# Inverse square roots of two layer norms: one GpSimd power instruction in place of an integer seed and Newton steps

## The chip, the core and the metric

The kernel runs on one core of a Trainium2 chip. Its time is device time in microseconds (us); the figure for a kernel is the median of its runs. A profile is one execution recorded by the hardware profiler; its times count from the start of its span. Engines are named as in the profile: PE (TensorE, matmuls), PEld (TensorE's weight loads), DVE (VectorE), ACT (ScalarE), POOL (GpSimd) and SP (SyncE, which issues nearly all transfers here).

## What is computed

One decode step of a transformer block: one row of 512 numbers, with two pieces. Piece A normalises the row, multiplies by wq to 32 query heads, attends over a cache of 16384 keys and values for 8 heads (four query heads share one), and multiplies by wo. Piece B normalises again and runs an MLP. With a sequence of length 1, the padded and shifted parts of B's mixer are all zero, so w1 and w2 have no effect and x1 is B's input.

```python
def _layernorm(x, axis=-1, eps=1e-5):
    m = jnp.mean(x, axis=axis, keepdims=True)
    v = jnp.var(x, axis=axis, keepdims=True)
    return (x - m) / jnp.sqrt(v + eps)
...
h = x + _A_ref(_layernorm(x, axis=-1), A_k_cache, A_v_cache, A_wq, A_wo)
h2 = h + _B_ref(_layernorm(h, axis=-1), B_w1, B_w2, B_w3, B_w4)
# _B_ref(x) comes down to: x + _gelu(_layernorm(x) @ w3) @ w4
```

In the second place two layer norms follow each other: B's input is the layer norm of h, and the MLP normalises that again. The mean of the second is zero and its variance is v/(v + eps), so both come from one variance v. The kernel keeps two inverse roots for it: number 0, of v + eps, for the residual (h + layernorm(h)), and number 1, of v(1 + eps) + eps², as the scale of the gelu's input.

## The kernel before, in words

**The stream.** SP issues every large transfer in a fixed order: wq (4 MB, into vb), then for four pairs of key/value heads the keys in two halves (kb[0], kb[1], 4 MB each) and the values (vb, 8 MB; the last pair's in two parts), then wo in four pieces (into kb[0]) and w3 in three and w4 in four pieces (into kb[1]). An issue waits until the buffer that it overwrites has been read: a key half until DVE has transposed it into kt (L609), a value block until PE has used it (L662), the first value block until the queries are computed from wq (L586). The pieces of w4 (`W4`) are row blocks 0 to 4, 5 to 9, 10 to 12 and 13 of 14.

**Start, first layer norm.** POOL makes an identity matrix (L545), DVE casts a corner of it (L550) and spreads it (L551), and PE uses it to bring x into rows of 128 on all partitions (L553). `row_sums` (L478) gives sum and sum of squares; `variance` (L496) the negative of the squared-mean difference, clamped; `seeds` (L505) adds epsilon (L513) and makes a first guess of the inverse root by integer arithmetic on the bits (L515, L518); `inverse_root` (L521) halves the argument (L528) and runs three Newton steps of two instructions each (L531, L533). All of it runs on DVE, on 128 partitions by 1 column. Meanwhile POOL clears two tiles, qb and pt (L560, L561). DVE then makes masks (L563 to L574) and, once wq has landed, the normalised input xn (L577), which starts the queries (L586).

**Attention.** For each pair DVE transposes the keys, PE forms the scores (L626), ACT takes the exponentials (L647), DVE transposes them (L651), and PE multiplies by the values (L662). POOL does nothing here but wait for the values (L448).

**End, second layer norm.** PE multiplies by wo (L728), DVE and PE fold the four partial rows (L732, L734), and `row_sums` forms h (tile hr) and its sums. ACT writes the centred row hc (L740); PE multiplies it by w3 (L746) without waiting for the scale. In that time DVE computes the variance, both arguments (L513 twice), both seeds and the Newton steps of root 1, and POOL the steps of root 0; POOL then forms xs = (h - mean) times root 0 (L753) and xsum = h + xs (L755). ACT's gelu (L758) needs the w3 product and root 1 as its scale; it runs in two halves, each transposed by DVE into hcol (L762). PE multiplies by w4 (L772), four matmuls for each of the 14 row blocks, block by block; ahead of block 10 it adds xsum through an identity matmul (L768). ACT writes the row (L777) and SP stores it (L778).

**Order.** Each engine runs its instructions in the order in which the program adds them. Semaphore waits are put in where an instruction reads or overwrites what another engine, or an earlier instruction of its own, has written. `dve`, `pool`, `act` and `pe` (L458 to L469) add an instruction to an engine's list.

Of the kernel before, what the change touches and what calls it, by code (L numbers as in the profile page):

```python
# [6 lines left out]
FP32 = mybir.dt.float32  # L7
BF16 = mybir.dt.bfloat16
I32 = mybir.dt.int32
ALU = mybir.AluOpType  # L10
# [331 lines left out]
def bass_sequential_preLN__gqa_block_cached__mixer_s_mlp__decode_kernel(  # L342
# [13 lines left out]
    with ExitStack() as ctx:  # L356
        sb = lambda name, shape, dt: ctx.enter_context(nc.sbuf_tensor(name, shape, dt))
# [26 lines left out]
        zd = sb("zd", [128, 32], FP32)  # L384
        scr = sb("scr", [128, 4], FP32)
        st = [sb(f"st{i}", [128, 16], FP32) for i in range(2)]
        sti = [sb(f"sti{i}", [128, 4], I32) for i in range(2)]
        xn = sb("xn", [128, NCH], BF16)
        qcol = sb("qcol", [128, 4, PAIRS * REP, 32], FP32)
        qb = sb("qb", [128, 4, PAIRS, QW], BF16)  # L390
# [15 lines left out]
        hr = sb("hr", [128, 128], FP32)  # L406
# [3 lines left out]
        xs = sb("xs", [128, 128], FP32)  # L410
        xsum = sb("xsum", [128, 128], FP32)
# [46 lines left out]
        def dve(fn, r=(), w=(), bank=()):  # L458
            return P.op("DVE", fn, r, w, bank)

        def act(fn, r=(), w=(), bank=()):
            return P.op("ACT", fn, r, w, bank)

        def pool(fn, r=(), w=(), bank=()):
            return P.op("POOL", fn, r, w, bank)
# [5 lines left out]
        def piece(cuts, m):  # L471
            return [lo <= m < hi for lo, hi in cuts].index(True)
# [23 lines left out]
        def variance(i):  # L496

            s, S = st[i], ("st", i)

            dve(lambda e: e.scalar_tensor_tensor(s[:, 2:3], s[:, 0:1], s[:, 0:1], s[:, 1:2],  # L500
                                                 ALU.mult, ALU.add), r=[(S, 0)], w=[(S, 2)])
            dve(lambda e: e.tensor_scalar(s[:, 3:4], s[:, 2:3], 0.0, -1.0, ALU.min, ALU.mult),
                r=[(S, 2)], w=[(S, 3)])

        def seeds(i, ns):  # L505


            s, t = st[i], sti[i]
            S, T = ("st", i), ("sti", i)
            lo, hi = min(ns), max(ns) + 1  # L510
            for n in ns:
                mul, add = (1.0 + EPS, EPS * EPS) if n else (1.0, EPS)
                dve(lambda e, n=n, mul=mul, add=add: e.tensor_scalar(s[:, 4 + n:5 + n], s[:, 3:4], mul, add,  # L513
                                                                     ALU.mult, ALU.add), r=[(S, 3)], w=[(S, 4 + n)])
            dve(lambda e: e.tensor_single_scalar(t[:, 2 + lo:2 + hi], s[:, 4 + lo:4 + hi].bitcast(I32), 1,  # L515
                                                 ALU.arith_shift_right),
                r=[(S, 4 + n) for n in ns], w=[(T, 2)])
            dve(lambda e: e.tensor_scalar(t[:, lo:hi], t[:, 2 + lo:2 + hi], -1, 1597463007,  # L518
                                          ALU.mult, ALU.add), r=[(T, 2)], w=[(T, n) for n in ns])

        def inverse_root(i, n, by):  # L521

            s, t = st[i], sti[i]
            S, T = ("st", i), ("sti", i)
            v, y = s[:, 4 + n:5 + n], t[:, n:n + 1].bitcast(FP32)
            z = s[:, 8 + n:9 + n]
            vh = s[:, 10 + n:11 + n]
            by(lambda e: e.tensor_scalar(vh, v, -0.5, None, ALU.mult), r=[(S, 4 + n)], w=[(S, 10 + n)])  # L528
            for k in range(3):
                dst, key = (s[:, 6 + n:7 + n], (S, 6 + n)) if k == 2 else (y, (T, n))  # L530
                by(lambda e: e.tensor_scalar(z, y, y, vh, ALU.mult, ALU.mult),  # L531
                   r=[(T, n), (S, 10 + n)], w=[(S, 8 + n)])
                by(lambda e, dst=dst: (e.scalar_tensor_tensor if by is dve else e.tensor_scalar)(  # L533
                    dst, z, 1.5, y, ALU.add, ALU.mult),
                   r=[(S, 8 + n), (T, n)], w=[key])


        load("x4", x4[:, :], A_x[0, 0:1, :].rearrange("o (q j) -> (o q) j", q=4), "x4", "ACT")
# [8 lines left out]
                                               channel_multiplier=1), r=["ident_f"], w=["ident_f"])  # L547


        dve(lambda e: e.tensor_copy(ident[:, :], ident_f[0:4, 0:4]), r=["ident_f"], w=["ident"])  # L550
        dve(lambda e: e.tensor_copy(quarter[:, :, :], ident[:, :].unsqueeze(2).to_broadcast([4, 4, 32])),  # L551
            r=["ident", "x4"], w=["quarter"])
        pe(lambda e: e.matmul(O_ps[0][:, 0:128], quarter[:, :, :].rearrange("p q u -> p (q u)"), x4[:, :],  # L553
                              start=True, stop=True), r=["quarter"], w=[("O", 0)], bank=[("O", 0)])
        row_sums(0, O_ps[0], ("O", 0))
        variance(0)
        seeds(0, (0,))
        inverse_root(0, 0, dve)
        act(lambda e: e.activation(scr[0:1, 0:1], mean4[0:1, 0:1], ACTF.Exp), r=["mean4"], w=["scr"])
        pool(lambda e: e.memset(qb[:, :, :, :], 0.0), w=["qb"])  # L560
        pool(lambda e: e.memset(pt[:, :, :, :, :], 0.0), w=["pt"])  # L561
# [2 lines left out]
            r=["ident_f"], w=["row32"])  # L564
        dve(lambda e: e.tensor_reduce(maskdd[:, :], ident_f[:, :].rearrange("p (n d) -> p d n", d=4), AX.X, ALU.add),
            r=["ident_f"], w=["maskdd"])
# [6 lines left out]
        for z, m, key, mk in ((zo, rowgh, "zo", "rowgh"), (zd, maskgh, "zd", "maskgh")):  # L573
# [5 lines left out]
            r=["hT", (("st", 0), 0), (("st", 0), 6)] + [("v", x) for x in range(VP)], w=["xn"])  # L579
# [3 lines left out]
        for i, key in enumerate(keys):  # L583
            P.part("query", i)
            for k in range(NCH):
                pe(lambda e, k=k: e.matmul(row[:, bass.ds(P.b, 512)], copies(xn[:, k:k + 1], 128),  # L586
                                           wq_k[:, k, bass.ds(P.c, REP * DH)], start=(k == 0), stop=(k == NCH - 1)),
                   r=["xn"], also=[("v", x) for x in range(VP)], w=["n" if key == "mn" else key], bank=[key])
        P.part()
        for g in range(2):  # L590
            half = banks[64 * g:64 * g + 64, PAIRS * g:PAIRS * g + PAIRS, :].rearrange("p j c -> p (j c)")
            for b in range(2):
# [3 lines left out]
                    r=["n" if x == "mn" else x for x in keys[PAIRS * g:PAIRS * g + PAIRS]], w=["qcol"],  # L596
                    bank=keys[PAIRS * g:PAIRS * g + PAIRS])
        for a in range(4):
            lo, hi, at = 32 * a, 32 * a + 32, QPAD + 32 * a
# [118 lines left out]
        for n, (lo, hi) in enumerate(W4):  # L718
# [4 lines left out]
            r=["o_m"], w=["o_f"])  # L723
        dve(lambda e: e.tensor_copy(o_b[:, :], o_f[:, :]), r=["o_f", ("r", 0, 0)], w=["o_b"])  # L724

        for r_ in range(32):
# [3 lines left out]
               r=["o_b"] + [("r", 0, n) for n in (piece(WO, r_),) if n], w=[("O", 0)], bank=[("O", 0)])  # L730
        h_ps, hkey = banks[:, 6, :], "spare0"
        dve(lambda e: e.tensor_copy(osum[:, :], O_ps[0][:, :]), r=[("O", 0)], w=["osum"], bank=[("O", 0)])  # L732
        for q in range(4):
            pe(lambda e, q=q: e.matmul(h_ps[32 * q:32 * q + 32, 0:128], copies(row32[:, 0:1], 32),  # L734
                                       osum[:, q * 128:(q + 1) * 128], start=True, stop=True),
               r=["osum", "row32"], w=[hkey], bank=[hkey])
        s = st[1]
        S = ("st", 1)
        row_sums(1, h_ps, hkey)
        act(lambda e: e.activation(hc[:, :, :], hT[:, :, :], ACTF.Identity, bias=s[:, 0:1], scale=1.0),  # L740
            r=["hT", (S, 0)] + [("r", 1, 0)], w=["hc"])


        for k in range(NCH):
            for q in range(4):
                pe(lambda e, k=k, q=q: e.matmul(s_ps[32 * q:32 * q + 32, 0, 0:FQ], hc[:, k, :],  # L746
                                                w3_sb[:, k, q * FQ:(q + 1) * FQ], start=(k == 0), stop=(k == NCH - 1)),
                   r=["hc"] + [("r", 1, n) for n in (piece(W3, k),) if n], w=[("s", 0)], bank=[("s", 0)])
        variance(1)
        seeds(1, (0, 1))  # L750
        inverse_root(1, 1, dve)
        inverse_root(1, 0, pool)
        pool(lambda e: e.tensor_scalar(xs[:, :], hr[:, :], s[:, 0:1], s[:, 6:7], ALU.add, ALU.mult),  # L753
            r=["hr", (S, 0), (S, 6)], w=["xs"])
        pool(lambda e: e.tensor_tensor(xsum[:, :], hr[:, :], xs[:, :], ALU.add), r=["hr", "xs"], w=["xsum"])  # L755
        for n in range(2):
            lo, hi = n * NHC // 2, (n + 1) * NHC // 2
            act(lambda e, lo=lo, hi=hi: e.activation(  # L758
# [7 lines left out]
        for m in range(NHC):  # L766
# [4 lines left out]
            for o in range(4):  # L771
# [4 lines left out]
                   r=[("hcol", 2 * m // NHC), ("r", 1, len(W3) + piece(W4, m))], w=["n"], bank=["mn"])  # L776
        act(lambda e: e.activation(fin[:, :], n_ps[:, 0:128], ACTF.Identity), r=["n"], w=["fin"], bank=["mn"])  # L777
        P.op("SP", lambda e: e.dma_start(out[0, 0:1, :].rearrange("o (q j) -> (o q) j", q=4), fin[0:128:32, :]),  # L778
             r=["fin"], w=["out"], dma="out")
# [32 lines left out]
```

## Time and profile before

| | |
|---|---|
| median of 3 runs | 191.78 us (191.37 to 191.93) |
| profiled execution, span | 190.4 us, 2182 instructions |
| what lies around the span | about 1.4 us (median less span; the profiled execution's own time is not listed apart) |
| PE busy | 118.6 us (62%) |
| DVE busy | 118.2 us (62%), 155 instructions |
| ACT busy | 9.3 us (5%) |
| POOL busy | 7.3 us (4%), 16 instructions |
| read from HBM | 79.17 MB, 416 GB/s over the span |

A row of the timeline gives start, duration, engine, line, operation, the tile written and the tiles read, the shape, and the number of instructions merged into it; in brackets stands the time that the engine was idle before it, and what ended that. A row of a group of instructions gives its busy time, the mean duration of one in ns, and its idle time with the releaser.

### The profile page before, as it was taken

The numbers are of one execution on the slowest core, as the hardware profiler recorded it, in microseconds if no ns is written. First come the engines' busy times: TensorE is split into PE (matmuls) and PEld (weight loads), VectorE is DVE, ScalarE is ACT, GpSimd is POOL, SyncE is SP. The second block draws the span as 40 slices with busy tenths as digits, with TensorE's granted clock in tenths as the row PEclk, the third lists the DMA queues.
The fourth block names the chain that finished last, engine by engine and source line by source line (L and its number), as shares of the span: only waits on it lengthen the run. The fifth ranks groups of instructions, "written<-read, shape, count | busy, mean of one in ns | idle before, by whom it ended". The sixth has DMA issues, their size and how long they took to land.

```text
span 190.4 us, 2182 instructions
## 1 busy us (share of the span) xinstructions
PE 118.6 (62%) x695; PEld 46.1 (24%) x695; DVE 118.2 (62%) x155; ACT 9.3 (5%) x16; POOL 7.3 (4%) x16
## 2 busy tenths in 40 slices
PE   0119709996195599940944989508449995294644
PEld 0103203442031143310311433203113332031212
DVE  6740799995504989845049989350479895504370
ACT  3000000000200000011000000020000000500020
POOL 7100000000000000000000000000000000000060
PEclk9999985899958579995585899975979999758855
DMA  6999999999999999997999999979999999989991
GB/s 227 434 441 441 441 441 441 441 441 441 413 441 406 420 523 441 441 441 330 441 441 441 523 441 413 441 324 420 413 441 441 441 441 441 441 367 421 409 411 51
DMA packets 3619, 79.20 MB, mean 416 GB/s; under 512 B 416, under 2 KB 544, under 8 KB 1568
## 3 DMA queue, kind: packets, MB, share of 16 engines
q1 hardware_dynamic: 3608, 79.17, 97.2%
q8 instruction: 1, 0.02, 0.0%
q14 instruction: 2, 0.02, 0.0%
q10 hardware_dynamic: 8, 0.00, 0.0%
HBM read 79.17 MB, written 0.00 MB: 416 GB/s over the span
## 4 chain that ended last, share of the span: by engine, by line
PE 39%; DMA 37%; DVE 16%; issue 4%; ACT 2%; ACTq 0%; SPq 0%; DVEq 0%
DMA kb<-in_A_k_cache_dram 31%; PE banks L626 22%; PE banks L662 6%; DMA vb<-in_A_wq_dram 6%; DVE kt L609 6%; PE banks L586 5%; DVE pt L651 3%; PE banks L728 2%; DVE mx L636 1%; ACT p_sb L647 1%; PE banks L620 1%; DVE od L681 1%; PE banks L772 1%; DVE qcol L593 1%; PE banks L639 1%
## 5 line engine op out<-in xcount | busy, mean ns | idle before, releaser
L609 DVE STREAM_TRANSPOSE kt<-kb 128x2048 int32<-128x2048 int32 (+1 forms) x37 | 71.3, 1987 | 4.3 <-DMA kb<-in_A_k_cache_dram 2.8
L626 PE MATMUL banks<-kt,qn 128*128 x256 | 68.7, 414 | 0.5
L626 PEld LDWEIGHTS banks<-kt,qn 128*128 x256 | 26.2, 102 | 41.4 <-issue 24.6
L662 PE MATMUL banks<-vb,pt 128*32 128x512 bf16 x256 | 24.4, 565 | 2.8 <-POOLq L448 2.8
L678 DVE TENSOR_SCALAR od<-banks,rowc 128x128 f32<-128x128 f32 x4 | 1.4, 350 | 26.3 <-PE banks L662 26.3
L620 PE MATMUL banks<-qn 128*128 128x512 bf16 x8 | 4.0, 495 | 17.3 <-DVE kt L609 17.1
L651 DVE STREAM_TRANSPOSE pt<-p_sb 64x1024 bf16<-64x1024 bf16 x8 | 9.9, 1239 | 5.4 <-ACT p_sb L647 5.3
L662 PEld LDWEIGHTS banks<-vb,pt 128*32 128x32 bf16 x256 | 9.0, 136 | 16.4 <-issue 12.4
L586 PE MATMUL banks<-vb,xn 128*128 x32 | 8.9, 446 | 6.1 <-DVE xn L577 6.1
L669 PE MATMUL banks<-acc,zd 128*32 128x1 f32 x8 | 1.1, 202 | 17.7 <-DVE pt L651 17.7
L647 ACT ACTIVATE p_sb<-banks,bias 128x1024 bf16<-128x1024 f32 x4 | 4.5, 1113 | 155.4 <-DVE nmh L643 155.4
L636 DVE TENSOR_REDUCE mx<-banks 128x1 f32<-128x1024 f32 x4 | 4.9, 1224 | 8.1 <-PE banks L626 8.1
L593 DVE STREAM_TRANSPOSE qcol<-banks 64x1024 f32<-64x1024 f32 x4 | 4.8, 1226 | 6.9 <-PE banks L586 6.9
L528 POOL TENSOR_SCALAR st<-st 128x1 f32<-128x1 f32 x1 | 0.2, 241 | 176.1 <-DVE st L513 176.1
L586 PEld LDWEIGHTS banks<-vb,xn 128*128 128x128 bf16 x32 | 3.6, 112 | 11.0 <-issue 8.5
L639 PE MATMUL banks<-mxd,mean 128*128 128x128 f32 x8 | 2.0, 326 | 6.6 <-DVE mxd L637 6.6
L620 PEld LDWEIGHTS banks<-qn 128*128 128x128 bf16 x8 | 0.8, 100 | 20.2 <-issue 20.0
L684 PE MATMUL banks<-od,zo 128*32 128x128 f32 x8 | 1.6, 285 | 6.5 <-DVE od L681 6.5
L669 PEld LDWEIGHTS banks<-acc,zd 128*32 128x32 f32 x8 | 0.7, 140 | 18.4 <-DVE pt L651 18.4
L681 DVE SCALAR_TENSOR_TENSOR od<-banks,rowc,od 128x128 f32<-128x128 f32 x12 | 4.2, 351 | 0.4
L550 DVE CAST ident<-ident_f 4x4 bf16<-4x4 f32 x1 | 3.8, 3848 | 0.6 <-POOL ident_f L545 0.6
L728 PE MATMUL banks<-kb,o_b 128*32 128x512 bf16 x32 | 3.5, 583 | 1.1 <-DVE o_b L724 1.1
(78 smaller groups left out, 44.6 us busy)
## 6 DMA issues: line engine op xcount, KB each, us to landing
kb<-in_A_k_cache_dram SPq DMA_DIRECT2D x8, 4096.0 KB, 29.7
vb<-in_A_v_cache_dram SPq DMA_DIRECT2D x2, 4096.0 KB, 29.2
vb<-in_A_wq_dram SPq DMA_DIRECT2D x1, 4096.0 KB, 12.3
kb<-in_A_wo_dram SPq DMA_DIRECT2D x2, 1536.0 KB, 25.4
kb<-in_B_w_dram SPq DMA_DIRECT2D x2, 640.0 KB, 25.4
kb<-in_B_w_dram SPq DMA_DIRECT2D x1, 896.0 KB, 22.4
kb<-in_B_w_dram SPq DMA_DIRECT2D x2, 448.0 KB, 23.4
kb<-in_A_wo_dram SPq DMA_DIRECT2D x1, 768.0 KB, 28.5
```

Source lines behind the costliest of these rows:

```text
L586: pe(lambda e, k=k: e.matmul(row[:, bass.ds(P.b, 512)], copies(xn[:, k:k + 1], 128), wq_k[:, k, bass.ds(P.c, REP * DH)], start=(k == 0), s ...
L593: dve(lambda e, g=g, b=b, half=half: e.transpose(qcol[64 * g:64 * g + 64, 2 * b:2 * b + 2, :, :].rearrange("p e m u -> p (e m u)"), half.r ...
L609: P.op("DVE", lambda e, view=view: e.transpose(view(kt), view(kb[y])), r=[("r", y, i) for i in range(RPARTS)], w=[("kt", t + i) for i in r ...
L620: pe(lambda e: e.matmul(row[:, bass.ds(P.y, 512)], copies(none, 128), copies(none, 512), start=True, stop=False, skip_group_check=True), r ...
L626: pe(lambda e, n=n: e.matmul(row[:, bass.ds(P.y, 512)], qn[:, n, bass.ds(P.q, 128)], key_piece(P.k, n), start=False, stop=(n == 3), skip_g ...
L636: dve(lambda e: e.tensor_reduce(mx[:, :], s_all, AX.X, ALU.max), r=[("s", 0), ("s", 1)], w=["mx"], **both)
L639: pe(lambda e: e.matmul(m_ps[:, 0:128], mean4[:, :], mxd[:, :], start=True, stop=True), r=["mxd", "mean4"], w=["m"], bank=["mn"])
L647: act(lambda e: e.activation(p_sb[:, :], s_all, ACTF.Exp, bias=bias[:, 0:1], scale=float(SCALE), accum_out=acc[:, :]), r=[("s", 0), ("s", ...
L651: dve(lambda e, g=g: e.transpose(pt[64 * g:64 * g + 64, :, :, g, :], p_sb[64 * g:64 * g + 64, :]), r=["p"], w=["pt"])
L662: pe(lambda e, l=l, ct=ct, ch=ch: e.matmul(O_ps[0][32 * ct:32 * ct + 32, :], pt[:, l, ch, :, :].rearrange("p g u -> p (g u)"), tiles[:, l ...
L681: dve(lambda e, block=block, c=c: e.scalar_tensor_tensor(od[:, :], block, rowc[:, c:c + 1], od[:, :], ALU.mult, ALU.add), r=[key, "rowc", ...
L728: pe(lambda e, r_=r_, q=q: e.matmul(O_ps[0][32 * q:32 * q + 32, :], copies(o_b[:, r_:r_ + 1], 32), wo_sb[:, r_ * D:(r_ + 1) * D], start=(r ...
```

## The change

The seeds and the Newton steps go, and with them the tile sti. `variance` now also makes the arguments, and one POOL instruction raises them to the power -0.5, with a tile of exponents (expo, 128x2, all -0.5, set by POOL at the start): 128x1 in the first layer norm, 128x2 in the second, where both roots come from one instruction. In the first layer norm that instruction stands on POOL ahead of the clearing of qb and pt. In the second, DVE forms xs as h - mean, without the root, and xsum as xs times root 0 plus h; POOL keeps only the power. The gelu and xsum wait for POOL. In the changed kernel the lines after the removed functions have smaller numbers.

```diff
-        sti = [sb(f"sti{i}", [128, 4], I32) for i in range(2)]
+        expo = sb("expo", [128, 2], FP32)
...
             dve(lambda e: e.tensor_scalar(s[:, 3:4], s[:, 2:3], 0.0, -1.0, ALU.min, ALU.mult),
                 r=[(S, 2)], w=[(S, 3)])
-        def seeds(i, ns):
...
+            for n in range(1 + i):
                 mul, add = (1.0 + EPS, EPS * EPS) if n else (1.0, EPS)
                 dve(lambda e, n=n, mul=mul, add=add: e.tensor_scalar(s[:, 4 + n:5 + n], s[:, 3:4], mul, add,
                                                                      ALU.mult, ALU.add), r=[(S, 3)], w=[(S, 4 + n)])
...
-        def inverse_root(i, n, by):
...
+            pool(lambda e: e.tensor_tensor(s[:, 6:7 + i], s[:, 4:5 + i], expo[:, 0:1 + i], ALU.pow),
+                 r=["expo"] + [(S, 4 + n) for n in range(1 + i)], w=[(S, 6 + n) for n in range(1 + i)])
...
+        pool(lambda e: e.memset(expo[:, :], -0.5), w=["expo"])
         dve(lambda e: e.tensor_copy(ident[:, :], ident_f[0:4, 0:4]), r=["ident_f"], w=["ident"])
...
         variance(0)
-        seeds(0, (0,))
-        inverse_root(0, 0, dve)
         act(lambda e: e.activation(scr[0:1, 0:1], mean4[0:1, 0:1], ACTF.Exp), r=["mean4"], w=["scr"])
         pool(lambda e: e.memset(qb[:, :, :, :], 0.0), w=["qb"])
         pool(lambda e: e.memset(pt[:, :, :, :, :], 0.0), w=["pt"])
...
         variance(1)
-        seeds(1, (0, 1))
-        inverse_root(1, 1, dve)
-        inverse_root(1, 0, pool)
-        pool(lambda e: e.tensor_scalar(xs[:, :], hr[:, :], s[:, 0:1], s[:, 6:7], ALU.add, ALU.mult),
-            r=["hr", (S, 0), (S, 6)], w=["xs"])
-        pool(lambda e: e.tensor_tensor(xsum[:, :], hr[:, :], xs[:, :], ALU.add), r=["hr", "xs"], w=["xsum"])
+        dve(lambda e: e.tensor_scalar(xs[:, :], hr[:, :], s[:, 0:1], None, ALU.add), r=["hr", (S, 0)], w=["xs"])
+        dve(lambda e: e.scalar_tensor_tensor(xsum[:, :], xs[:, :], s[:, 6:7], hr[:, :], ALU.mult, ALU.add),
+            r=["hr", "xs", (S, 6)], w=["xsum"])
```

More of the change, by code (lines that the diff above doesn't have):

```diff
@@ L503, in variance @@
                 r=[(S, 2)], w=[(S, 3)])
-        def seeds(i, ns):
[L508 to L511, printed above, removed]
+            for n in range(1 + i):
                 mul, add = (1.0 + EPS, EPS * EPS) if n else (1.0, EPS)
@@ L514, in seeds @@
                                                                      ALU.mult, ALU.add), r=[(S, 3)], w=[(S, 4 + n)])
[L515 to L519, printed above, removed]
-        def inverse_root(i, n, by):
[L523 to L535, printed above, removed]
+            pool(lambda e: e.tensor_tensor(s[:, 6:7 + i], s[:, 4:5 + i], expo[:, 0:1 + i], ALU.pow),
+                 r=["expo"] + [(S, 4 + n) for n in range(1 + i)], w=[(S, 6 + n) for n in range(1 + i)])
         load("x4", x4[:, :], A_x[0, 0:1, :].rearrange("o (q j) -> (o q) j", q=4), "x4", "ACT")
```

## The prediction

> **What bounds the kernel now.** I read the page first, for the span, the DMA row and the GB/s row.
>
> ```profile
> span 190.4 us, 2182 instructions
> DMA  6999999999999999997999999979999999989991
> GB/s 227 434 441 441 441 441 441 441 441 441 413 441 406 420 523 441 441 441 330 441 441 441 523 441 413 441 324 420 413 441 441 441 441 441 441 367 421 409 411 51
> ```
>
> The third line gives the DMA traffic in 40 slices of 4.76 us. After the start-up slice most slices stand near 440 GB/s (the lowest at 324), the 39th is still at 411, and only the last one falls to 51. The transfers run through from the first microseconds to within 4 us of the end: the kernel is a stream of 79 MB, and computation costs time only where it follows the last transfers. So the next view is the timeline of the tail, where the second layer norm lies. Columns are start, duration, engine, line and operation; in brackets, the engine's idle time before it and what ended that.
>
> ```profile
> 181.56 0.21 DVE L513 TENSOR_SCALAR st<-st 128x1 f32<-128x1 f32 x2
> 181.57 1.68 PE L746 MATMUL banks<-kb,hc 128*32 128x448 bf16 x16 [0.69 <-ACT hc L740]
> 181.80 0.24 POOL L528 TENSOR_SCALAR st<-st 128x1 f32<-128x1 f32 x1 [176.12 <-DVE st L513]
> 182.59 0.11 PEld L746 LDWEIGHTS banks<-kb,hc 128*32 128x32 bf16 x4 [0.52 <-DMA kb<-in_B_w_dram]
> 183.61 0.19 DVE L533 SCALAR_TENSOR_TENSOR st<-st,sti 128x1 f32<-128x1 f32 x1
> 183.89 0.85 ACT L758 ACTIVATE hg<-banks,st 128x224 bf16<-128x224 f32 x2 [2.37 <-DVE st L533]
> 184.33 0.26 POOL L533 TENSOR_SCALAR st<-st,sti 128x1 f32<-128x1 f32 x1
> 184.41 1.04 DVE L762 STREAM_TRANSPOSE hcol<-hg 128x224 bf16<-128x224 bf16 x2 [0.61 <-ACT hg L758]
> 185.04 0.46 PEld L772 LDWEIGHTS banks<-kb,hcol 128*32 128x32 bf16 x20 [2.33 <-DVE hcol L762]
> 185.04 1.45 PE L772 MATMUL banks<-kb,hcol 128*32 128x128 bf16 x40 [1.79 <-DVE hcol L762]
> 185.22 0.45 POOL L755 TENSOR_TENSOR xsum<-hr,xs 128x128 f32<-128x128 f32 x1
> 185.76 0.46 PEld L772 LDWEIGHTS banks<-kb,hcol 128*32 128x32 bf16 x20 [0.26 <-DMA kb<-in_B_w_dram]
> 186.41 0.50 PEld L768 LDWEIGHTS banks<-xsum,ident_f 128*128 128x128 f32 x2 [0.20 <-issue]
> 187.14 0.62 PE L772 MATMUL banks<-kb,hcol 128*32 128x128 bf16 x16
> 187.81 0.28 ACT L777 ACTIVATE fin<-banks 128x128 bf16<-128x128 f32 x1 [3.08 <-PE banks L772]
> 188.12 0.63 SPq L778 DMA_DIRECT2D out_dram<-fin  x1
> ```
>
> Three things are to be seen. First, the Newton steps do end a wait: L533 is done at 183.61 + 0.19 = 183.80 and the gelu (L758) starts 0.09 later, at 183.89, while the matmuls that it also needs (L746) end at 181.57 + 1.68 = 183.25. Second, a later wait ends on something else. The first 20 weight loads of L772 (blocks m = 0 to 4, four each) start at 185.04, but the next 20 (m = 5 to 9) start at 185.76 after 0.26 us idle that a transfer into kb ended: the second piece of W4 (blocks 5 to 9) had not landed. Third, from 185.76 nothing waits for the layer norm any more: 20 matmuls, the residual's matmul (L768, at 186.41; its operand xsum was ready at 185.22 + 0.45 = 185.67), the last 16 matmuls from 187.14, the last activation at 187.81, the output DMA at 188.12, and 190.4 - 188.12 = 2.3 us for that to finish.
>
> Are those transfers late because of the arithmetic, or because of the stream? Two more views answer it: the issues by line (the last two numbers are first and last start) and the windows of the tail (last two columns: DMA share and GB/s).
>
> ```profile
> L433 SPq DMA_DIRECT2D kb<-in_B_w_dram x7: 328/432/5845, 157.9 to 168.8; - x7
> 184.00:185.00 1.00, 0.00 (x0) 0.00 (x0) 0.59 (x2) 0.74 (x2) 0.80 (x3) 0.50 0.96 389
> 185.00:186.00 1.00, 0.96 (x32) 0.70 (x36) 0.45 (x1) 0.00 (x0) 0.59 (x2) 0.50 1.01 390
> 186.00:186.50 0.50, 0.50 (x21) 0.30 (x10) 0.00 (x0) 0.00 (x0) 0.00 (x0) 0.50 0.48 164
> 186.50:187.00 0.50, 0.50 (x2) 0.42 (x2) 0.00 (x0) 0.00 (x0) 0.00 (x0) 0.50 0.05 18
> ```
>
> All seven weight transfers of the second block were issued by 168.8, 17 us before the wait, and the DMA engines are still fully busy (0.96 and 1.01) while PE waits; they run empty in the half microsecond after 186. The landing at 185.7 is therefore set by the bytes ahead in the queue, and no edit of a layer norm moves it. That is the bound against which this change must be held.
>
> **The change, second layer norm.** Removed on DVE, after L513: L515, L518, L528 and three pairs L531/L533, nine instructions, from 181.56 + 0.21 = 181.77 to 183.80, 2.03 us. Removed on POOL: L528 and three pairs (n = 0), L753 and L755. Added: one POOL power over two columns, 128x2, which now stands alone between L513 and the gelu; call its duration P. DVE gets two 128x128 operations, xs (needs no root) and xsum (needs it).
>
> Start of the power: POOL's L528 started at 181.80, 0.09 after the first of the two L513 ended (181.56 + 0.15, by its row below), which is the one it needs; the power needs the second, so 181.77 + 0.09 = 181.86. Gelu start: 181.86 + P + 0.09 (the same handover as from DVE to ACT) = 181.95 + P, and not before 183.30 (end of L746 and 0.05).
>
> Gain side: at P up to 1.35 the gelu starts at 183.30, 0.59 sooner than now. Blocks 0 to 4 then run from 184.45, and PE waits for the second W4 piece 0.26 + 0.59 = 0.85 us instead of 0.26. Everything from 185.76 on stays. The whole 0.59 goes into that wait: gain 0.
>
> Loss side: the gelu may start 0.26 later than now, at 184.15, before blocks 5 to 9 start later. So the break-even is P = 184.15 - 181.95 = 2.20 us, and beyond it each microsecond of P is a microsecond of the kernel. DVE's new xsum waits for the power too, and ahead of hcol in the queue; it takes about 0.3 (L637 below has its shape), and the gelu's first half, which hcol waits for, takes 0.85/2 = 0.43 and its handover: the gelu covers it, barely. If it didn't, hcol would be some 0.1 us later, which the 0.26 takes up while P stays under about 2.1.
>
> How long is P? No power instruction stands in the trace. The nearest rows, with busy time and mean ns of one:
>
> ```profile
> L531 POOL TENSOR_SCALAR st<-sti,st 128x1 f32<-128x1 f32 x3 | 1.0, 340 | 0.4 <-DVE st L528 0.2
> L533 POOL TENSOR_SCALAR sti<-st,sti 128x1 f32<-128x1 f32 x2 | 0.5, 264 | 0.2
> L755 POOL TENSOR_TENSOR xsum<-hr,xs 128x128 f32<-128x128 f32 x1 | 0.5, 453 | 0.1
> L528 POOL TENSOR_SCALAR st<-st 128x1 f32<-128x1 f32 x1 | 0.2, 241 | 176.1 <-DVE st L513 176.1
> L531 DVE TENSOR_SCALAR st<-sti,st 128x1 f32<-128x1 f32 x6 | 1.6, 273 | 0.2
> L637 DVE TENSOR_SCALAR mxd<-ident_f,mx 128x128 f32<-128x128 f32 x4 | 1.1, 287 | 0.1
> L513 DVE TENSOR_SCALAR st<-st 128x1 f32<-128x1 f32 x3 | 0.4, 150 | 0.1
> ```
>
> Lower end: 0.24, one simple POOL instruction on one column (L528). Nearest in kind: 0.45, a POOL TENSOR_TENSOR over 128 columns (L755); the power has two columns, but more arithmetic in each. Upper end: the seven POOL steps that compute one root in the rows above run from 181.80 to 184.33 + 0.26 = 184.59, 2.79 us; a power done in software as laboriously, one column after the other, would take twice that, 5.6. I take 0.45, by the row that is of the same engine and instruction, and keep 0.24 and 5.6 for the range. The sum is 0 for every P up to 2.20; at 5.6 it is +3.4.
>
> One sharing could move the break-even: xs on DVE and the power on POOL become ready together. In the rows above a 128x128 TENSOR_SCALAR takes 287 ns and a 128x1 one (L513) 150: 137 ns for 127 more columns, about 1.08 ns each. I read that as one column per step, without a faster mode, so that xs leaves POOL alone and the break-even stays at 2.20.
>
> The Trainium skill, "SBUF — State Buffer", section "Who interferes with whom", says that a VectorE tensor_scalar between SBUF tensors can enter a mode that takes the port pair it shares with GpSimd, and that whichever starts first then blocks the other for its whole instruction; by that rule the power would start up to 0.29 late and the break-even would be 1.91. The skill's "VectorE: DVE Perf Modes", section "Side-by-side: where the cycles go for N=2048 bf16", puts an element at one cycle of 0.96 GHz without that mode, an estimate of 1.04 ns; the 1.08 of the rows agrees with it.
>
> **The change, first layer norm.** Nine DVE instructions leave here too, and the power (128x1) is put ahead of POOL's two memsets.
>
> ```profile
> 1.53 0.29 POOL L545 TENSOR_SCALAR_AFFINE_SELECT ident_f<-ident_f 128x128 f32<-128x128 f32 x1 [1.11 <-DVE ident_f L544]
> 1.76 2.18 POOL L560 MEMSET qb<- 128x2496 bf16 x1
> 1.86 3.85 DVE L550 CAST ident<-ident_f 4x4 bf16<-4x4 f32 x1 [0.57 <-POOL ident_f L545]
> 3.88 1.80 POOL L561 MEMSET pt<- 128x2048 bf16 x1
> 5.74 0.21 DVE L551 COPY quarter<-ident 4x128 bf16<-4x128 bf16 x1
> 8.29 0.15 DVE L513 TENSOR_SCALAR st<-st 128x1 f32<-128x1 f32 x1
> 11.47 0.17 DVE L574 COPY zd<-maskgh 128x32 f32<-128x32 f32 x1
> 13.00 0.29 DVE L577 TENSOR_SCALAR xn<-hT,st 128x4 bf16<-128x4 f32 x1 [1.35 <-DMA vb<-in_A_wq_dram]
> kb<-in_A_k_cache_dram SPq DMA_DIRECT2D x8, 4096.0 KB, 29.7
> ```
>
> The cast of a 4x4 tile (L550) takes 3.85 us: it starts at 1.86 and ends at 5.71, just as the second memset does (3.88 + 1.80 = 5.68). It was held by POOL. With the memsets behind the power it should take about 0.2, so the copy L551 starts near 2.1 instead of 5.74, and the variance is ready at 8.44 - 3.65 = 4.8 instead of 8.29 + 0.15. The power ends at 4.9 + P, the memsets (2.18 + 1.80) at 8.9 + P. None of this shortens the kernel: xn (L577) stands at 13.00 after 1.35 us idle that the landing of wq ended, and that landing does not move. The root has until 13.0, so the cover holds to P = 8; the memsets, which may now hold DVE's small copies or xn, are gone by 13.0 up to P = 4.1. Beyond that, xn is late by P - 4.1, at 5.6 by 1.5 us, and the first value load, issued when its queries end, by as much. A key transfer of 4096 KB stands 29.7 us from issue to landing (last line), of which its own bytes at 441 GB/s are 9.5: some 20 us of work lie ahead of it, so 1.5 us cost nothing. Term of the front: 0.
>
> **Sum.** 0 + 0 against the profiled execution, whose span is 190.4; the median of the runs, 191.78, lies 1.4 above that span for what lies around it. Forecast: 191.8. Of this kernel about 0.3% (0.58 us) can be told from no change.
>
> **The rivals.** *Slow power (slower).* Place: POOL between L513 and the gelu. Price: P - 2.20, deciding from P = 2.20 and measurable from 2.78, which is about the length of one root's steps on POOL now. At 4 us, between that and the upper end, it gives 193.6; at 5.6, 195.2. For it: POOL takes more than DVE for the same step (340 against 273 ns in L531), a power is more than a multiplication, and two columns are asked for. Against it: it is one dispatch, where the seven steps pay seven with a handover between each. Chance 0.42.
>
> *The stall is not what the view says (faster).* If the 0.26 us ahead of 185.76 were no DMA wait, the earlier gelu would come through: up to 0.59, so 191.2. For it: releasers are inferred. Against: the DMA engines are full up to just then, and the break falls exactly at the 20th weight load, where the second piece of W4 begins. Chance 0.06.
>
> *The change does nothing (no change).* This is my forecast: the removed wait is replaced by the wait for W4. Chance 0.52; its own range is 191.2 to 192.35.
>
> **How the numbers follow.** Same 0.52 (P up to 2.78, where the loss becomes measurable), slower 0.42 (P over 2.78), faster 0.06. For the 0.42 I have only that the break-even lies near the middle between 0.24 and 5.6, and that the row nearest in kind lies well below it. The range goes from 191.2 (the whole 0.59 comes through) to 195.0, short of the upper end's 195.2 by 0.2: some 0.15 is left above, for a power near that end or still slower, and 0.05 below.
>
> **What would show it.** In the changed profile: a POOL TENSOR_TENSOR of 128x2 under 2.2 us; the gelu near 183.3 instead of 183.89, released by PE or POOL; the second group of 20 weight loads of the w4 matmuls still at about 185.76 after a longer idle that DMA ended; the 4x4 cast at 0.2; xn still at 13.0. The forecast is wrong if the power takes over 2.2 (then that group starts after hcol without a DMA wait, and the span grows by the excess), or if the end moves earlier with the gelu.

## The result, and the profile after

The changed kernel takes 191.23 us (median of 10 runs, 190.92 to 191.42) against 191.78 us (median of 10 runs, 191.37 to 192.23): a ratio of 0.996, 95% interval 0.9948 to 0.9973. That is about 0.55 us faster, where no change was forecast. In the profiled executions the span goes from 190.4 to 189.9 us.

The timeline of the tail of the changed kernel, the rows that answer to those of before (lines 506, 719, 728, 742, 738, 747 and 748 are the former 513, 746, 758, 772, 768, 777 and 778; 508 is the power):

```profile
181.69 0.21 DVE L506 TENSOR_SCALAR st<-st 128x1 f32<-128x1 f32 x2
181.71 1.68 PE L719 MATMUL banks<-kb,hc 128*32 128x448 bf16 x16 [0.69 <-ACT hc L713]
181.83 0.28 DVE L723 TENSOR_SCALAR xs<-hr,st 128x128 f32<-128x128 f32 x1
181.99 0.70 POOL L508 TENSOR_TENSOR st<-st,expo 128x2 f32<-128x2 f32 x1 [172.13 <-DVE st L506]
...
182.81 0.35 DVE L724 SCALAR_TENSOR_TENSOR xsum<-xs,st,hr 128x128 f32<-128x128 f32 x1 [0.70 <-POOL st L508]
183.44 0.85 ACT L728 ACTIVATE hg<-banks,st 128x224 bf16<-128x224 f32 x2 [1.79 <-PE banks L719]
...
184.60 0.46 PEld L742 LDWEIGHTS banks<-kb,hcol 128*32 128x32 bf16 x20 [1.74 <-DVE hcol L732]
...
185.92 0.45 PEld L742 LDWEIGHTS banks<-kb,hcol 128*32 128x32 bf16 x20 [0.87 <-DMA kb<-in_B_w_dram]
...
186.57 0.50 PEld L738 LDWEIGHTS banks<-xsum,ident_f 128*128 128x128 f32 x2 [0.20 <-issue]
...
187.30 0.62 PE L742 MATMUL banks<-kb,hcol 128*32 128x128 bf16 x16
187.97 0.28 ACT L747 ACTIVATE fin<-banks 128x128 bf16<-128x128 f32 x1 [3.67 <-PE banks L742]
188.27 0.63 SPq L748 DMA_DIRECT2D out_dram<-fin  x1
```

Up to here the tail goes as the prediction had it. The power over two columns takes 0.70 us. The gelu starts at 183.44 instead of 183.89, released by PE and no longer by the layer norm. The second group of weight loads waits for its transfer 0.87 us instead of 0.26 and starts at 185.92, not sooner. The store is issued at 188.27, 0.15 us *later* than before, because every transfer from wq on lands about 0.15 us later in this execution (0.14 to 0.17 by the landings in the trace). So by the chain of work the kernel has gained nothing when it issues its store. The gain lies behind that point, where the prediction had looked at nothing. SP's own waits, of before and then of after, show it (us in total, times, longest):

```profile
SPq L780 <- DMA out_dram<-fin: 1.6, 1, 1.6
```
```profile
SPq L750 <- DMA out_dram<-fin: 1.0, 1, 1.0
```

The store of the same 1 KB takes 0.6 us less: from issue to the end of the span 190.4 - 188.12 = 2.3 us before, 189.9 - 188.27 = 1.6 after. The table of DMA queues says what else is different. First before, then after (queue, kind: packets, MB, share of the 16 engines):

```profile
q1 hardware_dynamic: 3608, 79.17, 97.2%
q8 instruction: 1, 0.02, 0.0%
q14 instruction: 2, 0.02, 0.0%
```
```profile
q1 hardware_dynamic: 3608, 79.17, 97.4%
q8 instruction: 1, 0.02, 0.0%
```

Two instruction fetches of about 8 KB on queue q14, 0.02 MB in all, are gone. One of them lay beside the store, as the queue table of the window from 188.5 to 190 us of the kernel before shows:

```profile
q14 instruction: 1, 0.01, 1.4%
q1 hardware_dynamic: 8, 0.00, 0.5%
```

The eight packets on q1 are the store. In the changed kernel the same window holds those eight packets alone.

The trace also has the time of every packet and of every landing. In the kernel before, the two fetches start at 186.57 and at 189.02; the second ends at 189.35. The store lands in four parts. Before, three of them land 1.61 to 1.62 us after the issue and the fourth 2.25 after it; in the changed kernel all four land 1.57 to 1.64 after it. So one part of four is late, not the whole store.

### The profile page after: what moved, and what is told of

Same layout as the page of the kernel before. It is cut to its first block, busy times and chain, and to the rows that moved or that the text cites. A ratio compares the mean times of both kernels' runs of the same rounds, so it can differ in the third digit from the quotient of the medians.

```text
span 189.9 us, 2162 instructions
## 1 busy us (share of the span) xinstructions
PE 118.5 (62%) x695; PEld 46.2 (24%) x695; DVE 115.0 (61%) x139; ACT 9.3 (5%) x16; POOL 5.7 (3%) x10
## 4 chain that ended last, share of the span: by engine, by line
DMA 65%; DVE 15%; PE 15%; issue 2%; SPq 1%; ACT 0%; DVEq 0%
DMA kb<-in_A_k_cache_dram 45%; DVE kt L582 14%; DMA kb<-in_B_w_dram 14%; PE banks L599 9%; DMA vb<-in_A_wq_dram 7%; PE banks L559 5%; SPq L433 1%; PE banks L742 1%; DVE qcol L566 1%; PE banks L593 1%; DVE qb L573 0%; PE banks L738 0%; DVE xn L550 0%; ACT fin L747 0%; DVEq L137 0%
## 5 line engine op out<-in xcount | busy, mean ns | idle before, releaser
L508 POOL TENSOR_TENSOR st<-st,expo 128x1 f32<-128x1 f32 (+1 forms) x2 | 1.3, 630 | 175.7 <-DVE st L506 175.7
L547 DVE COPY zo<-rowgh 128x32 f32<-128x32 f32 x1 | 3.6, 3629 | 0.0
```

What stands on the lines that cost most here:

```text
L547: dve(lambda e, z=z, m=m: e.tensor_copy(z[:, :].rearrange("p (n d) -> p n d", d=4), m[:, :, :].rearrange("p g h -> p (g h)").unsqueeze(2). ...
```

## The experiments

**Theory F**: the change makes VectorE's program shorter, and a shorter program does without an instruction fetch that held up the store. Counted in the programs as built, VectorE has 195 instructions before and 181 after, waits and branches included; POOL has 43 and 37. **Rival G**: the gelu's earlier start is the cause after all. **Rival H**: the start is the cause (the root of the first layer norm is ready at 5.99 instead of 10.39). The rows of the table are from each run's timing and from one profiled execution of it; the kernel before, run beside them, had medians of 191.97 to 191.99 us.

| | VectorE, POOL instructions | q14 fetches in the span | SP's wait for the store, us | median, us | ratio to before (95%) |
|---|---|---|---|---|---|
| before | 195, 43 | 2 | 1.6 | 191.78 | |
| after | 181, 37 | 0 | 1.0 | 191.23 | 0.9960 (0.9948 to 0.9973) |
| e1 | 195, 37 | 2 | 1.6 | 191.90 | 0.9992 (0.9981 to 1.0004) |
| e2 | 181, 43 | 0 | 1.0 | 191.23 | 0.9961 (0.9948 to 0.9975) |
| e3 | 187, 46 | 0 | 1.0 | 191.34 | 0.9968 (0.9956 to 0.9980) |
| e4 | 189, 36 | 0 | 1.0 | 191.38 | 0.9973 (0.9963 to 0.9983) |
| e5 | 211, 37 | 1, in the middle | 1.0 | 191.86 | 0.9992 (0.9983 to 1.0002) |
| e6 | 189, 51 | 0 | 1.0 | 191.34 | 0.9965 (0.9952 to 0.9978) |
| e7 | 181, 41 | 0 | 1.0 | 193.13 | 1.0046 (1.0027 to 1.0065) |
| e8 | 181, 37 | 0 | 1.0 | 191.02 | 0.9949 (0.9932 to 0.9966) |
| e9 | 192, 37 | 2 | 1.7 | 191.81 | 0.9989 (0.9978 to 1.0001) |
| e10 | 203, 37 | 2 | 1.9 | 191.82 | 0.9989 (0.9977 to 1.0001) |
| e11 | 227, 37 | 1, in the middle | 1.0 | 191.82 | 0.9994 (0.9984 to 1.0005) |

### e1 and e2: the old length again, on one engine each

e1, in the changed kernel ahead of xn, with a tile of its own (padd):

```diff
+        for i in range(14):
+            dve(lambda e, i=i: e.memset(padd[:, i:i + 1], 0.0))
```

> The changed kernel with 14 more VectorE instructions (memsets of single columns of an unused tile) in VectorE's idle time before xn, so that VectorE's program is as long as in the kernel before; POOL's is not. Theory F (the program's length): the kernel before ends late because an instruction fetch of 8 KB runs on the transfer engines beside the output store; a shorter VectorE program does without it. Expected: the page shows q14 instruction fetches again, the store takes about 2.3 us from issue to the end of the span instead of 1.7, and the time is that of the kernel before, 191.8 (ratio 1.000 within 0.002). Rival G (the earlier gelu): the gain comes from the second layer norm's shorter wait by some route that the chain doesn't show: then 14 instructions in idle time cost nothing, 191.2 (ratio 0.997). Rival H (the start): the first layer norm's 3 us earlier end is the cause: 191.2 too.

e2, at the same place:

```diff
+        for i in range(6):
+            pool(lambda e, i=i: e.memset(padp[:, i:i + 1], 0.0))
```

> The changed kernel with 6 more POOL instructions (memsets of single columns of an unused tile) behind the clearing of pt, so that POOL's program is as long as in the kernel before; VectorE's is not. Theory F with VectorE's program as the one that counts: no fetch, 191.2 (ratio 0.997). Theory F with POOL's program as the one that counts: fetches as before, 191.8 (ratio 1.000). Rivals G and H: 191.2.

The 14 instructions of e1 do nothing that anyone waits for: the timeline of e1 has them at 0.23 us together, ahead of 3.46 us in which VectorE waits for wq.

```profile
9.45 0.23 DVE L552 MEMSET padd<- 128x1 f32 x14
13.13 0.29 DVE L553 TENSOR_SCALAR xn<-hT,st 128x4 bf16<-128x4 f32 x1 [3.46 <-DMA vb<-in_A_wq_dram]
```
```profile
SPq L753 <- DMA out_dram<-fin: 1.6, 1, 1.6
```
```profile
q8 instruction: 1, 0.02, 0.0%
q14 instruction: 2, 0.02, 0.0%
```

Yet the whole gain is gone (0.9992), with both fetches and the slow store back. e2 keeps the gain. So it hangs on the length of VectorE's program, not on POOL's, and not on the work of either layer norm: G and H both expected e1 at 191.2.

### e3 and e4: each layer norm alone

e3 is the kernel before with the power in the first layer norm only, e4 with the power in the second only (with the new xs and xsum).

```diff
 # e3
-        seeds(0, (0,))
-        inverse_root(0, 0, dve)
+        dve(lambda e: e.tensor_scalar(s0[:, 4:5], s0[:, 3:4], 1.0, EPS, ALU.mult, ALU.add),
+            r=[(("st", 0), 3)], w=[(("st", 0), 4)])
+        pool(lambda e: e.tensor_tensor(s0[:, 6:7], s0[:, 4:5], expo[:, 0:1], ALU.pow),
+             r=["expo", (("st", 0), 4)], w=[(("st", 0), 6)])
 # e4
-        seeds(1, (0, 1))
-        inverse_root(1, 1, dve)
-        inverse_root(1, 0, pool)
...
+        pool(lambda e: e.tensor_tensor(s[:, 6:8], s[:, 4:6], expo[:, 0:2], ALU.pow),
+             r=["expo", (S, 4), (S, 5)], w=[(S, 6), (S, 7)])
```

> The kernel before with the power in the first layer norm alone; the second keeps seeds and Newton steps. VectorE's program is 8 instructions shorter than before, POOL's 3 longer. Theory F: if 8 fewer VectorE instructions are enough, no q14 fetch near the end and 191.2 (ratio 0.997), with the gelu still at about 183.9; if not, 191.8. Rival G: 191.8, because the gelu is as late as before. Rival H: 191.2, because the start is as early as in the changed kernel.

> The kernel before with the power in the second layer norm alone; the first keeps seed and Newton steps on VectorE. VectorE's program is 6 instructions shorter than before, POOL's 7 shorter. Theory F: if 6 fewer VectorE instructions are enough, no q14 fetch near the end and 191.2 (ratio 0.997); if not, 191.8 although the gelu starts near 183.4. Rival G: 191.2. Rival H: 191.8.

Each half alone brings most of the gain: 0.9968 and 0.9973, intervals that overlap that of the whole change. The two gains don't add, as two savings on a path would; either half takes VectorE's program below the point at which the fetches begin. In e3 the gelu is still released by the Newton steps, so that G falls a second time; in e4 the start is as before (the cast takes 3.89 us, the Newton steps end at 10.44), and so does H.

### e6: the gain without the power

The kernel before, with one word changed:

```diff
-        inverse_root(0, 0, dve)
+        inverse_root(0, 0, pool)
```

> The kernel before, with the seven instructions of the first layer norm's Newton steps on POOL instead of VectorE; no power anywhere, and the start about 1 us later, within the wait for wq. VectorE's program is 6 instructions shorter than before, as in e4. Theory F: no q14 fetch near the end, 191.2 (ratio 0.997). A theory in which the power itself, the earlier gelu or the earlier start is the cause: 191.8 (ratio 1.000).

Ratio 0.9965: seven Newton instructions moved from VectorE to POOL, no power anywhere, and the same gain. One condition came out otherwise than expected: with the Newton steps ahead of POOL's memsets the cast takes 0.16 us and the root is ready at 7.67, which is 2.7 us earlier than before and not 1 us later. So e6 speaks against the power and the earlier gelu, not against the earlier start; that is settled by e1 and e4. (Its profiled execution, at 192.04 us, is the slowest of its ten runs, with transfers late from the middle on; I take only its start, its queues and its store from it.) The power is not the cause of the gain; it is one way to shorten VectorE's program.

### e7: what a slow power would have cost

```diff
+            for k in range(4 * i):
+                pool(lambda e, k=k: e.tensor_tensor(padp[:, 2 * k:2 * k + 2], s[:, 4:6], expo[:, 0:2], ALU.pow),
+                     r=["expo", (S, 4), (S, 5)])
             pool(lambda e: e.tensor_tensor(s[:, 6:7 + i], s[:, 4:5 + i], expo[:, 0:1 + i], ALU.pow),
```

> The changed kernel with four more powers of the same shape ahead of the one of the second layer norm, into an unused tile: the gelu waits for five powers, some 3 us, instead of 0.7. If the wait for the second piece of W4 hides what the gelu loses up to 0.87 us beyond the present start (183.44), the gelu at about 182.0 + 5 x 0.65 + 0.1 = 185.3 is 1.9 us late and costs 1.9 - 0.87 = 1.0 us: 192.3 (ratio 1.002 to the kernel before). If the gelu were on the path without cover, it would cost 1.9 us: 193.1 (1.007).

The timeline of e7, the four further powers, the real one and what waits for it:

```profile
182.14 2.65 POOL L510 TENSOR_TENSOR padp<-st,expo 128x2 f32<-128x2 f32 x4 [172.69 <-DVE st L507]
184.76 0.69 POOL L512 TENSOR_TENSOR st<-st,expo 128x2 f32<-128x2 f32 x1
185.54 0.85 ACT L732 ACTIVATE hg<-banks,st 128x224 bf16<-128x224 f32 x2 [3.73 <-POOL st L512]
...
186.70 0.99 PEld L746 LDWEIGHTS banks<-kb,hcol 128*32 128x32 bf16 x40 [3.71 <-DVE hcol L736]
...
189.59 0.62 SPq L752 DMA_DIRECT2D out_dram<-fin  x1
```

Here no transfer ends a wait of the w4 matmuls: they run from 186.70 in one piece. The gelu is 185.54 - 183.44 = 2.10 us later than in the changed kernel, the issue of the store 189.59 - 188.27 = 1.32. The wait for W4 has hidden 0.78, near the 0.87 that stood there, and the rest comes through one to one. The median, 193.13, is 1.9 us above the changed kernel's, which by itself is what the theory without cover forecast (193.1); the trace decides against that one. In the profiled execution the span is only 1.3 longer (191.2 against 189.9). The other 0.6 lies outside the span: what lies there varies from 1.3 to 2.3 us over the executions of e7, and from 1.3 to 1.5 in the other runs. The 16 KB fetch on queue q8, which starts between 187.0 and 188.1 in the other traces, starts at 192.51 in this one, behind the span; whether it makes the difference is not shown.

### e8: the identity matmul in the gap

```diff
-            if m == W4[-2][0]:
+            if m == W4[1][0]:
                 pe(lambda e: e.matmul(n_ps[:, 0:128], ident_f[:, :], xsum[:, :], start=False, stop=False,
                                       skip_group_check=True), r=["ident_f", "xsum"], w=["n"], bank=["mn"])
+            if m == W4[-2][0]:
                 pe(None)
```

> The changed kernel with the residual's identity matmul (0.73 us of PE) ahead of w4's block 5 instead of block 10, that is, into the 0.87 us in which PE waits for the second piece of W4. If that landing and not the layer norm sets the end, the matmuls after it run without the 0.73, held at the last only by the landings of the third and fourth pieces (186.84 and 187.16 in the changed kernel's trace): the end comes about 0.35 us earlier, 190.9 (ratio 0.995 to the kernel before). If the landing doesn't set the end: 191.2 (ratio 0.997).

```profile
184.90 0.46 PEld L743 LDWEIGHTS banks<-kb,hcol 128*32 128x32 bf16 x20 [1.99 <-DVE hcol L732]
...
185.56 0.50 PEld L738 LDWEIGHTS banks<-xsum,ident_f 128*128 128x128 f32 x2 [0.20 <-issue]
...
186.28 0.46 PEld L743 LDWEIGHTS banks<-kb,hcol 128*32 128x32 bf16 x20 [0.22 <-issue]
...
186.93 0.45 PEld L743 LDWEIGHTS banks<-kb,hcol 128*32 128x32 bf16 x16 [0.20 <-DMA kb<-in_B_w_dram]
187.62 0.28 ACT L748 ACTIVATE fin<-banks 128x128 bf16<-128x128 f32 x1 [3.02 <-PE banks L743]
187.92 0.62 SPq L749 DMA_DIRECT2D out_dram<-fin  x1
```

PE does the identity matmul at 185.56, while the second piece of W4 is still on its way (it lands at 185.93), goes on at 186.28, and waits again only for the third piece of W4 (186.93). The store is issued at 187.92, 0.35 us sooner than in the changed kernel, as expected. The median, 191.02, is the lowest of the study: 0.9949 of before (0.9932 to 0.9966). Against the changed kernel's 0.9960 the intervals overlap, so that the step from one to the other is shown by the trace and only probable by the times. This is where the time that the power freed can be spent.

### e5, e9, e10, e11: longer and longer

All are the changed kernel with more memsets of one column on VectorE: e9 11 ahead of xn; e10, e5 and e11 14 there and 8, 16 and 32 behind the making of o_b, while VectorE waits for the wo matmuls. (The expectation of e11 says 48 and 34; its edit adds 14 + 32 = 46, 32 more instructions than before.)

```diff
+        for i in range(16):
+            dve(lambda e, i=i: e.memset(padd[:, 32 + i:32 + i + 1], 0.0))
         h_ps, hkey = banks[:, 6, :], "spare0"
```

> The changed kernel with 30 more VectorE instructions (memsets of single columns of an unused tile): 14 before xn as in e1, and 16 while VectorE waits for the wo matmuls. Its VectorE program is the longest of all, 16 instructions longer than before. Theory F, with collision in time: the fetches are set off when VectorE gets to a fixed place of its program, so here some 16 instructions earlier, and both are over before the output store at 188.3; the page shows two q14 instruction fetches, the store takes 1.7 us to the end of the span, and the time is 191.2 (ratio 0.997). Rival F2 (a longer VectorE program costs by itself, wherever its fetches lie, for instance in what comes after the last instruction): 191.8 (ratio 1.000).

> The changed kernel with 11 more VectorE instructions before xn: its VectorE program is 3 instructions shorter than in the kernel before and 3 longer than in e4. So far 6 fewer than before went without a fetch, and as many as before had two at the end. If the place that sets off the fetch lies above this length: no q14 fetch, 191.2 (ratio 0.997 to the kernel before); if below: two q14 fetches, a store of 2.2 us, 191.8 (1.000).

> The changed kernel with 22 more VectorE instructions, 8 more than the kernel before has, half as far beyond it as e5. If a fetch of 8 KB costs half a microsecond wherever it lies (at the end through the store, in the middle through the transfers, as e5's single profile suggests): one or two q14 fetches in the span and 191.8 (ratio 1.000). If e5's loss in mid-stream had another cause and a fetch costs only beside the store: 191.2 (0.997) where the fetches lie before the store, 191.8 where they lie beside it.

> The changed kernel with 48 more VectorE instructions, 34 more than the kernel before has: 14 before xn, 34 while VectorE waits for the wo matmuls. If the cost goes with the fetches and not with the instructions: as many fetches as in e5 (one, in the middle) and the same time, 191.8 (ratio 1.000), with all landings after the fetch about 0.45 us later than in the changed kernel. If each further instruction costs: 192.3 or more (1.003).

e5 refutes theory F in its first form, which had the cost in the store alone: its store is as fast as in the changed kernel (1.0), and it is no faster than the kernel before. Its page shows one q14 fetch, and that lies neither at the end nor beside the store. The queue table of its window from 43 to 44 us:

```profile
q1 hardware_dynamic: 12, 0.79, 181.4%
q14 instruction: 1, 0.01, 1.9%
```

From there the transfers of e5 are late. xn starts at 13.17 in e5 and at 13.24 in the changed kernel, so wq landed no later; but the second group of loads, which waits for the second piece of W4, starts at 186.37 in e5, at 186.49 in e11 and at 185.92 in the changed kernel. e5, then e11:

```profile
186.37 0.46 PEld L747 LDWEIGHTS banks<-kb,hcol 128*32 128x32 bf16 x20 [0.19 <-DMA kb<-in_B_w_dram]
```
```profile
186.49 0.46 PEld L747 LDWEIGHTS banks<-kb,hcol 128*32 128x32 bf16 x20 [0.62 <-DMA kb<-in_B_w_dram]
```

The landings in the trace show where the time goes. A large transfer lands in sixteen parts. In e5 the last part lands 0.11 to 0.12 us behind the fifteenth in the transfers up to 32.5 us, and 0.49 to 0.56 behind it in every one from 52.4 on; in e11, 0.01 to 0.03 and then 0.76 to 0.82. No other run has a step of more than about 0.2. So one part of sixteen falls behind around the fetch (it starts at 43.71 in e5, at 43.84 in e11) and does not catch up, and whoever needs the transfer waits for that part: in e5 fifteen parts of the second piece of W4 have landed by 185.81, the last at 186.33, and the loads start at 186.37.

The transfers are what bounds this kernel, so what one part of each has lost at 44 us is lost at the end. e11, with 16 more instructions than e5, costs the same (0.9994 against 0.9992), with the same single fetch in the middle: it is the fetch that costs, not the instruction. e10, with 203 instructions, has again two fetches in the span and the slow store (1.9), and loses as much; e9, with 192, too.

## Why the prediction was wrong

**The bound in the tail: right.** The forecast was that a gelu 0.59 us sooner would only lengthen the wait for the second piece of W4, to 0.85. Measured: 0.45 sooner, and 0.87. e7 shows the other side, late gelu hidden up to 0.78, and e8 that the gap is real. But the forecast took the cover from one execution, and the traces show that it varies: the gelu, released by the w3 matmuls, starts at 183.23 in e9 and at 184.33 in e4, where the wait for the second piece of W4 is down to 0.19. In the profiled execution of e3, which keeps the Newton steps of the second layer norm, it starts at 184.35, and the timeline shows no wait of the w4 matmuls that a transfer ended:

```profile
184.35 0.85 ACT L763 ACTIVATE hg<-banks,st 128x224 bf16<-128x224 f32 x2 [2.38 <-DVE st L534]
185.50 1.02 PEld L777 LDWEIGHTS banks<-kb,hcol 128*32 128x32 bf16 x40 [2.50 <-DVE hcol L767]
```

In such an execution an earlier gelu can be worth something. How often that happens is open; it is little in the median, since e3 and e6 have nearly the whole gain without an earlier gelu (191.34 against 191.23).

**The power: cheap, as taken.** Taken were 0.45 us; measured are 0.70 over two columns and 0.56 over one. Both lie far below the break-even of 2.20, so the rival of the slow power, at 0.42, did not come. Its price was sized well: the five powers of e7 last from 182.14 to 185.45, 3.31 us, for which the sum gives 3.31 - 2.20 = 1.11 against the kernel before. The store was issued 1.47 later than before, of which 0.29 is the later end of the arguments (182.06 instead of 181.77); that leaves 1.18.

**VectorE beside the power: right.** xs runs from 181.83 to 182.11 with the power starting at 181.99, 0.09 after its arguments: neither holds the other.

**The start: right in its effect.** The cast fell from 3.85 us to 0.16, and the memsets now hold the copies zo and zd instead (3.63 us in the row below, 0.18 before). The row of the copy is one of the changed kernel's timeline of the start:

```profile
1.87 0.16 DVE L525 CAST ident<-ident_f 4x4 bf16<-4x4 f32 x1 [0.57 <-POOL expo L524]
2.58 0.21 DVE L526 COPY quarter<-ident 4x128 bf16<-4x128 bf16 x1 [0.56 <-DMA x<-in_A_x_dram]
5.43 0.56 POOL L508 TENSOR_TENSOR st<-st,expo 128x1 f32<-128x1 f32 x1 [3.55 <-DVE st L506]
...
6.26 3.63 DVE L547 COPY zo<-rowgh 128x32 f32<-128x32 f32 x1
...
13.24 0.29 DVE L550 TENSOR_SCALAR xn<-hT,st 128x4 bf16<-128x4 f32 x1 [3.33 <-DMA vb<-in_A_wq_dram]
```

One wait was overlooked: the copy L526 starts at 2.58, not at 2.1, since x itself had not landed. All of it ends in the wait for wq. The Trainium skill, "SBUF — State Buffer", section "Who interferes with whom", says that a VectorE copy or cast can, under conditions on its operands, enter a mode in which it needs the port pair shared with GpSimd, and that whichever starts first then blocks the other for its whole instruction; the trace agrees for the memsets with the cast before and the copies after. For xs and the power it shows no such hold.

**The step that failed** is the sum: "0 + 0", with "2.3 us for that to finish" taken as a constant behind the last activation. That term was not constant: it went to 1.6, with the fetch beside it gone, and gave -0.6, of which 0.15 went to later transfers. I counted what the removed instructions cost where they run, on VectorE and on POOL, and not that they have to be brought in, by transfers beside the stream and the store. The page of the profile showed it: a row q14 of kind "instruction" with two packets in the queue table, two bytes in ten thousand of the traffic, in a kernel whose end is a transfer. My rival for a faster kernel, at 0.06, named the right time, 191.2, by a mechanism that the trace of after excludes.

The Trainium skill, "Runtime: NRT & Kernel Launch", section "Instruction fetch mechanics", has an engine's sequencer fetch the next block of its program by a DMA queue of its own while it runs the current one, and calls the cost mostly hidden. The runs agree that fetches are transfers beside the kernel's own; that they are hidden does not hold here, where one costs about 0.5 us.

**What is shown and what is not.** Shown, by lengthening and by shortening VectorE's program in kernels that are otherwise alike: up to 189 instructions there is no q14 fetch in the span, from 192 on there is, and with it go about 0.5 us. Shown by the landings: with a fetch at the end one of the store's four parts is late (2.25 us after the issue in before, 2.21 in e1, 2.36 in e9, 2.55 in e10), while the other three, and all four in the runs without such a fetch, land by 1.65; with a fetch in the middle one part of sixteen of every later transfer is late. Argued only: that the late part stands behind the fetch on one transfer engine, since the trace does not name a packet's engine. It fits that in e9 and e10 the last of the store's packets of 256 bytes starts just where the fetch ends (189.47 and 189.70), 0.18 and 0.26 us behind the one ahead of it. In before and e1 the packets start together, and only a landing is late; and no run has its last fetch near the end but clear of the store. Open: why a program of 192 to 203 instructions has its fetches at the end and one of 211 or 227 has one at 44 us, and why a part loses more (0.44 us in e5, 0.77 in e11) than the 0.31 us that the fetch's packet takes.

## What to carry to other kernels

Where transfers bound a kernel, an instruction fetch is a transfer too: look in the queue table for rows of kind "instruction" within the span, and count the instructions of the engine concerned before and after a change, also of those that run in idle time. A term that stands behind the last instruction of the chain, such as the store, is part of the sum and has causes of its own. An engine made faster ahead of a wait for a transfer gives nothing by itself, but it opens a gap that other work can be moved into.

## What the runs showed of the hardware

- A POOL power of a 128x1 tile takes 0.56 us and of a 128x2 tile 0.70, less than a third of the seven Newton instructions on POOL (2.79 us from first to last).
- A fetch of about 8 KB costs this kernel about 0.5 us whether it lies beside the last store or in mid-stream, though it is one part in ten thousand of the bytes. What is late is one part of the store's four, or one of each later transfer's sixteen.
- 14 memsets of one column on VectorE take 0.23 us together (e1), and 46 of them cost no more than 11, each with its fetch or fetches (e11 against e9, both 191.8).
